# Fourier filter and SoLU network: filter products on VectorE in the first steps, weights prepared later, first sums ahead of loads

## The chip, the cores and the metric

The kernel runs on one core of a Trainium2 chip. The metric is the time of one execution on the device, in microseconds; the time of a kernel is the median over several runs. Besides, one execution of each kernel was taken by the hardware profiler, and all durations of single instructions come from such an execution.

## The reference

All data are 32-bit floats outside; x has 8 sequences of 3136 positions with 256 channels.

```
X = rfft(x, axis=1);  Y = X * (filt_r + 1j * filt_i)
y = irfft(Y, n=3136, axis=1)            # (8, 3136, 256) -> 25088 tokens of 256
h = y @ w_in                            # 256 -> 1024
sm = exp(h - max(h)) / (sum(exp(h - max(h))) + 1e-9)
solu = h * sm
ln = (solu - mean) / sqrt(var + 1e-6) * g_ln
out = ln @ w_out                        # 1024 -> 256
```

## The kernel before

**Transforms.** A sequence of 3136 = 49 x 64 positions is transformed in two stages with a pass through memory between them. For sequence 1 the first stage (L221) is done in 8 pieces of x; its results go to the memory tensor d (GpSimd issues the stores, L227). The second stage goes by units i = 0 to 6: a fetch of t from d (SP's queue, L286), the forward matmuls (L296, into two PSUM tiles pb), the product with the filter f (loaded by GpSimd's queue, L636), the inverse matmuls (L296 again, into pc, read from pr and pi), ScalarE's copy to g, and a store. From sequence 2 on the first stage works on a sum and a difference of two halves of x: diff on VectorE (L249), the sum on GpSimd (L255), matmuls at L264. Tables de come by ScalarE's queue (L677). At the end, matmuls (L367, L390) bring the data back into y, which stays in SBUF for two sequences.

**The filter product.** `multiply(i, part, add)` computes one part of the complex product: two multiplications on VectorE, each with one input in PSUM (L317, L318), then an add or subtract of two SBUF tensors (L319) on the engine that `add` names. Part 0 gives pr, part 1 gives pi; both use the same tile pt for the second term. Odd units of sequence 1 use spare room in y for t, f, pr, pi, pt, de and g, so their rows are named y.

**The network.** Tokens are taken in blocks of 128, two blocks (a pair) at a time. Both matrix products use seven block products instead of eight (Strassen's scheme in Winograd's form), so they need sums of inputs: `pair_sums` makes four sums of y on GpSimd (s, L696), `project_sums` those of solu (u, L696). `product(j, m)` is product m of pair j (L717); its PSUM banks are read by ScalarE (`keep`, L727) and by VectorE (`finish`, L741 and L738, which also track the row minimum nmax). Product 4 accumulates into the bank that `finish` of the same step reads first, and product 7 needs the bank that `finish` in the even step frees, so both wait for L741. Then `exponential` (ScalarE, L749), `normalize` (VectorE, L760 to L765), `turn` (a transpose in blocks of 32 on VectorE, L781), `square` (ScalarE, L773), `regroup` (SP's queue moves the transposed data into solu_t, L793), `deviations` (GpSimd, L800, L802) and, from step 9 on, `project` (L838).

**Order.** The order on every engine is written out by hand. `step(k)` emits one step; an even step k = 2j does products 1, 2, 6, 7 of pair j, an odd one products 5, 3, 4. Lists of jobs by step (`early`, `middle`, `late`, `stores`, `loads`, `products`, `first_parts`, `second_parts`) hang the work of the transforms into it. For sequence 1 the units 0 to 6 stand at steps t = 4, 5, 6, 7, 8, 10, 12 (`PLAN`): forward at t, part 0 of the product at the end of t, part 1 in step t + 1 (ahead of `turn` or after `normalize`), inverse late in t + 1. Fetches of t, de and f stand two steps ahead, f of odd units one step. LAG is 9: for t + 1 < 9, that is units 0 to 3, the add of `multiply` is on GpSimd; later, and for all other sequences, on VectorE.

**Before the steps.** The network's weights are given as 64-bit floats and converted by integer operations on VectorE (`load_float64`, L418 to L440) with a last add on GpSimd (L442), eight pieces in all, number 7 the last. `prepare_w_out` then works on w_out in four parts at the ends of steps 0 to 3: (0) scale by g_ln on VectorE (L654), (1) a mean by matmuls with ones (L662) and a copy to w_bar, (2) subtract w_bar on VectorE (L667), (3) the sums for Strassen's scheme on VectorE (`weight_sums`, L145). The tiles ones and w_bar take the buffers of pr and pi. The first reader of the finished w_out is `project` in step 9.

Loads of x whose step would be below 0 are issued at once while the lists are built, so ahead of everything in the steps; these are the two pieces 6 and 7 of sequence 1, four DMA issues on GpSimd's queue (L210). The first `pair_sums(0)` follows them in that queue.

Of the kernel before, what the change touches and what calls it, by code (L numbers as in the profile page):

```python
# [12 lines left out]
ALU = mybir.AluOpType  # L13
# [20 lines left out]
LAG = 9  # L34
# [60 lines left out]
def kernel(  # L95
# [10 lines left out]
    nc = tc.nc  # L106
# [72 lines left out]
    class Spectrum:  # L179
# [125 lines left out]
                                 t2[block, u::2, :])  # L305
            self.spectra[i] = pss

        def multiply(self, i, part, add):

            residues, w = self.shape(i)  # L310
            rows = slice(0, NQ * residues)
            f = self.fs[i][rows, 0:w]

            out, term = (self.buffer(i, kind, [P, 2, C])[rows, 0:w, :]
                         for kind in (("pr", "pi")[part], "pt"))
            re, im = (ps[rows, 0:w, :] for ps in self.spectra[i])
            nc.vector.tensor_tensor(out=out, in0=re, in1=f[:, :, part, :], op=ALU.mult)  # L317
            nc.vector.tensor_tensor(out=term, in0=im, in1=f[:, :, 1 - part, :], op=ALU.mult)  # L318
            add(out=out, in0=out, in1=term, op=(ALU.subtract, ALU.add)[part])  # L319
            self.prods.setdefault(i, []).append(out)  # L320
            if part == 1:
                del self.fs[i], self.spectra[i]
# [74 lines left out]
    with ExitStack() as st:  # L397
# [10 lines left out]
                in_=src)  # L408
            return raw

        def load_float64(dst, raw, negate, share):


            lo, hi = raw[:, :, 0], raw[:, :, 1]
            power = wpool.tile([P, 512], I32, name="power", tag="power", bufs=2)
            frac = dst.bitcast(I32)
            ts, stt = nc.vector.tensor_scalar, nc.vector.scalar_tensor_tensor
            ts(out=lo, in0=lo, scalar1=8, scalar2=None, op0=ALU.logical_shift_right)  # L418
            rest = lo.bitcast(FP32)
            ts(out=power, in0=hi, scalar1=20, scalar2=0x7FF, op0=ALU.logical_shift_right,  # L420
               op1=ALU.bitwise_and)
            ts(out=power, in0=power, scalar1=896.0, scalar2=0.0, op0=ALU.subtract, op1=ALU.max)
            if negate:
                ts(out=power, in0=power, scalar1=255.0, scalar2=None, op0=ALU.min)
                ts(out=power, in0=power, scalar1=23, scalar2=-2 ** 31, op0=ALU.logical_shift_left,
                   op1=ALU.bitwise_or)
            else:
                ts(out=power, in0=power, scalar1=255.0, scalar2=2.0 ** 23, op0=ALU.min, op1=ALU.mult)
            stt(out=power, in0=hi, scalar=-2 ** 31, in1=power, op0=ALU.bitwise_and,
                op1=ALU.bitwise_xor)  # L430
            ts(out=frac, in0=hi, scalar1=0xFFFFF, scalar2=3, op0=ALU.bitwise_and,
               op1=ALU.logical_shift_left)
            nc.vector.tensor_tensor(out=frac, in0=frac, in1=power, op=ALU.bitwise_or)


            if share:
                nc.scalar.mul(rest, lo, 2.0 ** -44)
                nc.gpsimd.tensor_tensor(out=rest, in0=rest, in1=power.bitcast(FP32), op=ALU.mult)
            else:
                stt(out=rest, in0=lo, scalar=2.0 ** -44, in1=power.bitcast(FP32), op0=ALU.mult,  # L440
                    op1=ALU.mult)
            nc.gpsimd.tensor_tensor(out=dst, in0=dst, in1=rest, op=ALU.add)  # L442

        filters, tables = {}, {}

# [23 lines left out]
        weights = []  # L469
# [17 lines left out]
        sp = Spectrum(0, pools, resident(filters), resident(tables))  # L487
        raws = {}
# [47 lines left out]
        idle_row(8, "idle")  # L536

        def convert(j):
            load_float64(weights[j][0], raws.pop(j), negate=j < 4, share=j < 4)

        for j in range(2):
            convert(j)
# [9 lines left out]
        for n in range(16):  # L552
            (nc.sync, nc.scalar)[n % 2].dma_start(
                out=t2_0[NH * (n % 4):NH * (n % 4) + NH, n // 4, :], in_=rows_x[n:n + 1])
# [29 lines left out]
        for i0, n, rows in ((0, 4, P), (4, 4, P), (8, NP - 9, P), (NP - 1, 1, NQ)):  # L584
            f, at = filters[i0]
            nc.sync.dma_start(
                out=f_dram[i0:i0 + n].rearrange("i u q k c -> (u q) i (k c)")[0:rows],
# [104 lines left out]
    def tokens(k, c):  # L692
        return y[:, c, P * (k % NT):P * (k % NT) + P]
# [4 lines left out]
    def pair_sums(j):  # L698

        s14 = upool.tile([P, 2, P], FP32, name=f"s14_{j}", tag="s14")  # L700
        s23 = wk.tile([P, 2, P], FP32, name=f"s23_{j}", tag="s23")
        sums[j] = s1, s2, s3, s4 = s14[:, 0, :], s23[:, 0, :], s23[:, 1, :], s14[:, 1, :]
        a11, a12, a21, a22 = (tokens(2 * j + i, c) for i in range(2) for c in range(KD))
        sum_of(s1, a21, a22, ALU.add)
        sum_of(s2, s1, a11, ALU.subtract)
        sum_of(s3, a11, a21, ALU.subtract)
        sum_of(s4, a12, s2, ALU.subtract)
# [164 lines left out]
    def ahead(t, by):  # L872
        return loads[max(0, t - by)]

    row_loads = []

    for e in range(1, B):
        first_at, spectrum_at, back_at = PLAN[e]
        sp = Spectrum(e, pools, load_filter, load_de)
        if e == 1:  # L880
            sp = second
            sp.load, sp.load_de = load_filter, load_de
        for i, t in enumerate(first_at):
            dma = nc.gpsimd.dma_start
            if e == 1:
                if i not in sp.xs:
                    row_loads.append((t, t - 1, -1, lambda sp=sp, i=i, dma=dma: sp.fetch_x(i, [dma] * 2)))
                for u in range(2):
                    (early, late)[u][t].append(lambda sp=sp, i=i, u=u: sp.first(
                        i, (u,), psum(f"pa_{sp.e}_{i}_{u}").rearrange("p a c -> p (a c)").rearrange(  # L890
                            "p (o n) -> p o n", o=1), nc.scalar.copy, sp.xs[i][0:NK, 2 * u:2 * u + 2, :]))
                    (early, late)[u][t].append(lambda sp=sp, i=i, u=u: sp.store_first(
                        i, 2 * u, nc.gpsimd.dma_start))
            else:

                row_loads.append((t, t - 2, -1, lambda sp=sp, i=i: sp.fetch_quarters(i, nc.sync.dma_start)))
                stores[t].append(lambda sp=sp, i=i: sp.difference(i))
                products[t].append(lambda sp=sp, i=i: sp.sum(i))
                late[t].append(lambda sp=sp, i=i: sp.first_quarters(
                    i, [psum(f"pa_{sp.e}_{i}_{g}") for g in range(2)]))  # L900
                stores[t + 1].append(lambda sp=sp, i=i, dma=dma: sp.store_quarters(i, dma))
        for i, t in enumerate(spectrum_at):

            other = e == 1 and i % 2 == 1 and t + 1 < LAG
            add = nc.gpsimd.tensor_tensor if t + 1 < LAG else nc.vector.tensor_tensor


            dma = nc.sync.dma_start if e == 1 else nc.scalar.dma_start
            ahead(t, 2).append(lambda sp=sp, i=i, dma=dma: sp.fetch(i, dma))
            ahead(t, 1 if e == 1 and i % 2 == 1 else 2).append(lambda sp=sp, i=i: sp.fetch_filter(i))  # L910
            ahead(t, 2).append(lambda sp=sp, i=i: sp.fetch_de(i))
            early[t].append(lambda sp=sp, i=i, o=other: sp.forward(i, psum_pair(f"pb_{sp.e}_{i}", o)))
            first_parts[t].append(lambda sp=sp, i=i, add=add: sp.multiply(i, 0, add))
            second_parts[t + 1].append(lambda sp=sp, i=i, add=add: sp.multiply(i, 1, add))
            late[t + 1].append(lambda sp=sp, i=i, o=other: sp.inverse(i, psum_pair(f"pc_{sp.e}_{i}", o)))
            stores[t + 2].append(lambda sp=sp, i=i: sp.store(i, nc.gpsimd.dma_start))


        assert S * (e - 1) <= P * (back_at[0] // 2 * 2) and P * (back_at[-1] + 2) <= S * e // P // 2 * 2 * P
        for ch, t in enumerate(back_at):  # L920
            row_loads.append((
                t, t - 1, spectrum_at[-1] + 2, lambda e=e, ch=ch: fetch_back(e, ch)))
            second_one = ch and t == back_at[ch - 1]
            (late if second_one else early)[t].append(lambda e=e, ch=ch: back_halves(
                e, ch, [psum(f"py_{e}_{ch}_{g}") for g in range(2)]))
            (late if second_one else middle)[t].append(lambda e=e, ch=ch: join_halves(e, ch))
    row_loads.sort(key=lambda load: load[0])
    for n, (t, latest, earliest, load) in enumerate(row_loads):


        at = max(t - 3, earliest, min(row_loads[n - 4][0] + 1, latest) if n >= 4 else -1)
        assert at < t
        if at < 0:
            load()
        else:
            loads[at].append(load)

# [2 lines left out]
    def step(k):  # L940
        j, odd = divmod(k, 2)
# [90 lines left out]
                job()  # L1032
        for job in late[k] + loads[k]:
            job()
        if k < 4:
            prepare_w_out(k)

    with tc.manual_schedule():
        pair_sums(0)
        for k in range(blocks + LAG):  # L1040
            step(k)

# [29 lines left out]
```

## Time and profile before

| | us |
|---|---|
| median of 6 runs (1636.37 to 1645.49) | 1640.63 |
| the profiled execution | 1628.72 |
| its span, first to last instruction | 1626.9 |
| TensorE busy | 1551.3 |
| VectorE busy | 1294.6 |
| GpSimd busy | 1130.8 |
| ScalarE busy | 901.7 |
| first product of step 0 starts (L717) | 105.34 |
| step 4 starts | 147.84 |
| step 9 starts | 200.37 |

In the profile's rows a line such as L296 is the line of the kernel that issued the instruction; the tiles written and read stand as out<-in; xN counts instructions that were merged. In a timeline the first two numbers are the start and the time that the row covers, and a bracket at the end gives the idle time of the engine before it and what ended it. In a row of a group, the numbers between bars are the sum of the durations in us and the mean in ns, and then the idle time before them. SPq and the like are queues from which an engine issues DMAs.

### The profile page before, as it was taken

What the parts mean: (1) busy time and instruction counts of PE and PEld (TensorE: products, weight loads), DVE (VectorE), ACT (ScalarE), POOL (GpSimd) and SP (SyncE); (2) the same over time, 40 slices, a digit from 0 to 9 for tenths busy, and PEclk for the clock granted to TensorE, in tenths of its full rate; (3) what the DMA queues carried; (4) which work ended last, traced back from release to release, by engine and by line L of the source; (5) the groups of instructions that cost most, each with busy time, mean ns of one, the idle gap of its engine ahead of it and who ended that gap; (6) DMA issues with size and microseconds to landing.
All of it is one profiled execution on the core that took longest, in us unless ns stands there. A gap on an engine that the chain in (4) does not pass through costs nothing. (4 is left out here: it accounts for less than half of the span.)

```text
span 1626.9 us, 36975 instructions
## 1 busy us (share of the span) xinstructions
PE 1551.3 (95%) x12710; PEld 1048.9 (64%) x12710; DVE 1294.6 (80%) x2633; ACT 901.7 (55%) x1772; POOL 1130.8 (70%) x1325
## 2 busy tenths in 40 slices
PE   5888799999999999999999999999999999999997
PEld 1353366666766676666766676666776777777776
DVE  1676598898899889887989789877888777777772
ACT  2134465566565665566656655566656555666562
POOL 4444687678777877697588867778576766676764
PEclk8999899999999999999999999999999999999999
DMA  9888768877888779866787678866785455444443
GB/s 271 252 258 246 214 205 223 235 222 193 207 241 241 196 182 248 229 190 174 203 248 208 178 190 232 229 178 170 204 230 160 122 132 127 102 111 111 105 111 98
DMA packets 377805, 312.13 MB, mean 192 GB/s; under 512 B 63322, under 2 KB 343395, under 8 KB 377619
## 3 DMA queue, kind: packets, MB, share of 16 engines
q1 hardware_dynamic: 306260, 169.81, 40.7%
q0 software_dynamic: 34464, 101.68, 20.6%
q10 hardware_dynamic: 36896, 38.28, 7.9%
q8 instruction: 103, 1.69, 0.5%
q14 instruction: 82, 0.67, 0.1%
HBM read 124.86 MB, written 81.50 MB: 127 GB/s over the span
## 5 line engine op out<-in xcount | busy, mean ns | idle before, releaser
L838 PEld LDWEIGHTS o<-w_out_sb,solu_t 128*128 128x128 f32 x3136 | 382.0, 193 | 48.2 <-issue 43.0
L838 PE MATMUL o<-w_out_sb,solu_t 128*128 128x128 f32 x3136 | 400.6, 276 | 3.1 <-DVE ot L854 2.7
L838 PEld LDWEIGHTS o<-w_out_sb,u 128*128 128x128 f32 x2352 | 308.1, 192 | 145.0 <-issue 104.8
L717 PE MATMUL m<-w_in_sb,s 128*128 128x512 f32 x784 | 395.9, 607 | 5.1 <-POOL s L696 1.6
L838 PE MATMUL o<-w_out_sb,u 128*128 128x128 f32 x2352 | 312.1, 276 | 8.5 <-ACT ot L850 5.9
L717 PE MATMUL m<-w_in_sb,y 128*128 128x512 f32 x588 | 309.5, 610 | 6.4 <-DVE nmax L741 4.4
L696 POOL TENSOR_TENSOR u<-solu_t 128x512 f32<-128x512 f32 x98 | 133.5, 1363 | 248.2 <-DMA solu_t<-turn 166.2
L727 ACT COPY h<-m 128x512 f32<-128x512 f32 x294 | 173.0, 589 | 238.2 <-PE m L717 214.8
L765 DVE SCALAR_TENSOR_TENSOR h<-e,rsum,h 128x1024 f32<-128x1024 f32 x196 | 287.3, 1466 | 6.9
L850 ACT ACTIVATE ot<-o,rs_t 128x128 f32<-128x128 f32 x392 | 143.8, 367 | 257.3 <-PE o L838 245.5
L741 DVE CUSTOM_DVE_ANT_0 h<-m,h 128x512 f32<-128x512 f32 x196 | 134.3, 685 | 162.6 <-ACT h L727 106.2
L773 ACT ACTIVATE h<-h,nmu 128x1024 f32<-128x1024 f32 x196 | 225.0, 1148 | 46.9 <-DVE turn L781 45.8
L781 DVE STREAM_TRANSPOSE turn<-h 128x1024 f32<-128x1024 f32 x196 | 243.1, 1240 | 3.2
L749 ACT ACTIVATE e<-h,nmax 128x1024 f32<-128x1024 f32 x196 | 225.3, 1150 | 5.0 <-DVE h L765 4.9
L717 PEld LDWEIGHTS m<-w_in_sb,s 128*128 128x128 f32 x784 | 128.7, 191 | 92.4 <-issue 81.6
L696 POOL TENSOR_TENSOR u<-solu_t,u 128x512 f32<-128x512 f32 x98 | 142.0, 1449 | 42.9 <-PE o L838 36.7
L717 PEld LDWEIGHTS m<-w_in_sb,y 128*128 128x128 f32 x588 | 96.5, 192 | 106.1 <-issue 54.5
L854 DVE SCALAR_TENSOR_TENSOR ot<-o,rs_t,ot 128x128 f32<-128x128 f32 x294 | 102.1, 347 | 78.7 <-ACT ot L850 57.0
L696 POOL TENSOR_TENSOR solu_t<-solu_t,solu_t 128x512 f32<-128x512 f32 x98 | 152.4, 1555 | 7.7
L696 POOL TENSOR_TENSOR u<-u,solu_t 128x512 f32<-128x512 f32 x98 | 133.4, 1361 | 0.6
L696 POOL TENSOR_TENSOR s<-y 128x128 f32<-128x128 f32 x196 | 100.8, 514 | 0.5
L367 PEld LDWEIGHTS py<-wb_t,t 50*64 50x64 f32 x3584 | 57.7, 135 | 43.3 <-issue 19.4
(113 smaller groups left out, 1971.4 us busy)
## 6 DMA issues: line engine op xcount, KB each, us to landing
solu_t<-turn SPq DMA_DIRECT2D x784, 128.0 KB
out_dram<-ot SPq DMA_DIRECT2D x196, 128.0 KB
t<-d POOLq DMA_DIRECT2D x112, 200.0 KB, 4.4
d<-x POOLq DMA_DIRECT2D x100, 200.0 KB, 5.2
f<-f_dram POOLq DMA_DIRECT2D x39, 512.0 KB, 7.7
d<-g POOLq DMA_DIRECT2D x39, 512.0 KB, 5.4
t<-d ACTq DMA_DIRECT2D x36, 512.0 KB
x<-in_x_dram SPq DMA_DIRECT2D x112, 98.0 KB
```

The lines of the kernel that those rows point to most:

```text
L367: nc.tensor.matmul(out=views[g][64 * h:64 * h + 64, cb, i, :], lhsT=t4[rows, i, c0:c0 + 64], rhs=wb_t[rows, 0:N1], start=True, stop=True)
L696: nc.gpsimd.tensor_tensor(out=out, in0=in0, in1=in1, op=op)
L717: nc.tensor.matmul(out=ms[j, bank], lhsT=lhsT, rhs=w_in_sb[:, w, :], start=m in (1, 2, 7), stop=True, skip_group_check=True)
L727: nc.scalar.copy(out=h_half(k, i), in_=ms[j, 0])
L741: nc.vector.tensor_tensor_reduce(out=h_half(k, i), in0=ms[j, bank], in1=h_half(*kept), scale=1.0, scalar=sofar, op0=ALU.add, op1=ALU.min, ...
L749: nc.scalar.activation(out=e, in_=hs[k], func=AFT.Exp, bias=nmaxs.pop(k)[:, 1:2], scale=-1.0, accum_out=esum)
L765: nc.vector.scalar_tensor_tensor(out=solu, in0=e, scalar=rsum, in1=solu, op0=ALU.mult, op1=ALU.mult, accum_out=nmu)
L773: nc.scalar.activation(out=solu, in_=solu, func=AFT.Square, bias=nmu, scale=-float(DFF), accum_out=variances[g][:, i:i + 1])
L781: nc.vector.transpose(out=turns[g][:, :, i, :], in_=solus[k].rearrange("p (f j) -> p f j", j=32))
L838: nc.tensor.matmul(out=pos[p, bank], lhsT=lhs[:, f, :], rhs=w[:, f, :], start=f == 0 and m in (1, 2, 7), stop=True, skip_group_check=True)
L850: nc.scalar.activation(out=out_half(p, *to)[0], in_=pos[p, 0], func=AFT.Copy, scale=rs)
L854: nc.vector.scalar_tensor_tensor(out=ot, in0=pos[p, bank], scalar=rs, in1=out_half(p, *kept)[0], op0=ALU.mult, op1=ALU.add)
```

## The change

Three things are changed, all of them in steps 0 to 9 or just ahead of them.

1. For units 0 to 3 of sequence 1, part 1 of the filter product is emitted directly after part 0, at the end of step t, and both adds are on VectorE. Units from 4 on, and the other sequences, stay as they were.
2. The parts of `prepare_w_out` stand at the ends of steps 0, 1, 3 and 5 instead of 0, 1, 2 and 3.
3. `pair_sums(0)` is emitted ahead of the two early loads of x, and the last add of weight piece 7 is on VectorE.

The instructions of TensorE, ScalarE and SP keep their order; GpSimd loses nine adds, and VectorE gains nine.

```diff
-        def multiply(self, i, part, add):
+        def multiply(self, i, part, add=nc.vector.tensor_tensor):
...
-        def load_float64(dst, raw, negate, share):
+        def load_float64(dst, raw, negate, share, add=nc.gpsimd.tensor_tensor):
...
-            nc.gpsimd.tensor_tensor(out=dst, in0=dst, in1=rest, op=ALU.add)
+            add(out=dst, in0=dst, in1=rest, op=ALU.add)
...
-            load_float64(weights[j][0], raws.pop(j), negate=j < 4, share=j < 4)
+            load_float64(weights[j][0], raws.pop(j), negate=j < 4, share=j < 4,
+                         add=(nc.vector if j == 7 else nc.gpsimd).tensor_tensor)
...
-    row_loads = []
+    row_loads, first_loads = [], []
...
-            add = nc.gpsimd.tensor_tensor if t + 1 < LAG else nc.vector.tensor_tensor
...
-            first_parts[t].append(lambda sp=sp, i=i, add=add: sp.multiply(i, 0, add))
-            second_parts[t + 1].append(lambda sp=sp, i=i, add=add: sp.multiply(i, 1, add))
+            first_parts[t].append(lambda sp=sp, i=i: sp.multiply(i, 0))
+            (first_parts[t] if t + 1 < LAG else second_parts[t + 1]).append(
+                lambda sp=sp, i=i: sp.multiply(i, 1))
...
-            load()
+            first_loads.append(load)
...
-        if k < 4:
-            prepare_w_out(k)
+        if k in (0, 1, 3, 5):
+            prepare_w_out((k + 1) // 2)
...
         pair_sums(0)
+        for load in first_loads:
+            load()
         for k in range(blocks + LAG):
```

## The prediction

> **What bounds it now.** I read the whole page first, then a table of stretches, then TensorE's timeline where the table shows a hole, then VectorE's and GpSimd's over the same time. (In the page's rows PE is TensorE, DVE VectorE, ACT ScalarE, POOL GpSimd.)
>
> ```profile
> PE 1551.3 (95%) x12710; PEld 1048.9 (64%) x12710; DVE 1294.6 (80%) x2633; ACT 901.7 (55%) x1772; POOL 1130.8 (70%) x1325
> PE   5888799999999999999999999999999999999997
> PEclk8999899999999999999999999999999999999999
> ```
>
> TensorE bounds the kernel: 95% busy, and from the sixth slice on (203 us) nothing is left to win. The change acts in steps 0 to 9, which lie between 105 and 203 us. There the table of stretches shows the holes (busy us of PE, PEld, DVE, ACT, POOL, then granted clock, DMA share, GB/s):
>
> ```profile
> 100.00:120.00 20.00, 16.29 (x68) 9.07 (x67) 13.75 (x34) 6.91 (x13) 10.04 (x15) 0.83 0.77 271
> 140.00:160.00 20.00, 15.87 (x68) 5.01 (x67) 19.46 (x40) 9.89 (x17) 8.21 (x11) 0.91 0.83 227
> 160.00:180.00 20.00, 15.02 (x78) 6.29 (x78) 12.12 (x25) 9.01 (x17) 15.05 (x18) 0.91 0.66 200
> 180.00:200.00 20.00, 12.83 (x63) 5.33 (x64) 13.21 (x24) 6.83 (x12) 13.43 (x15) 0.83 0.83 264
> 147.84:200.37 52.53, 38.49 (x200) 15.50 (x197) 37.75 (x71) 22.76 (x40) 33.73 (x37) 0.90 0.75 229
> 200.37:252.90 52.53, 51.95 (x334) 33.52 (x333) 44.91 (x89) 33.23 (x66) 43.40 (x52) 1.00 0.69 201
> ```
>
> In 147.84 to 200.37 us (start of step 4 to start of step 9) TensorE idles 14 us; right after, 0.6 us. No engine is full there, so these are waits in a chain. TensorE's timeline names them (in brackets the idle time and its releaser):
>
> ```profile
> 114.84 3.78 PE L717 MATMUL m<-w_in_sb,s 128*128 128x512 f32 x4 [1.63 <-POOL s L696]
> 144.20 2.07 PE L717 MATMUL m<-w_in_sb,y 128*128 128x512 f32 x2 [1.48 <-DVE nmax L741]
> 153.09 2.34 PE L717 MATMUL m<-w_in_sb,s 128*128 128x512 f32 x4 [1.17 <-DVE rsum L760]
> 164.25 0.44 PE L296 MATMUL pc<-pi,de 64*64 64x256 f32 x2 [4.85 <-POOL pi L319]
> 186.74 0.70 PE L296 MATMUL pc<-pi,de 64*64 64x256 f32 x2 [5.44 <-POOL pi L319]
> 197.43 1.58 PE L296 MATMUL pc<-y 64*64 64x256 f32 x8 [1.40 <-DVE y L317]
> ```
>
> So: the first sum of y comes late; step 3 waits for VectorE; twice the inverse transform waits for the last add of the filter product, which stands on GpSimd behind two loads of f, one sum of x and four sums of y. The stalls cost a second time through the clock: the granted clock is 0.50 in 113.4 to 120.2, 144.1 to 147.5, 164.6 to 168.0 and 185.0 to 191.9 us. TensorE at half speed for the parts of these in which it works loses about 2.7, 1.6, 1.7 and 2.6 us.
>
> VectorE meanwhile has holes of its own, because TensorE is late:
>
> ```profile
> 169.91 0.69 DVE L741 CUSTOM_DVE_ANT_0 h<-m,h 128x512 f32<-128x512 f32 x1 [5.30 <-PE m L717]
> 177.82 0.69 DVE L741 CUSTOM_DVE_ANT_0 h<-m,h 128x512 f32<-128x512 f32 x1 [2.30 <-ACT h L727]
> 193.22 0.69 DVE L741 CUSTOM_DVE_ANT_0 h<-m,h 128x512 f32<-128x512 f32 x1 [6.48 <-PE m L717]
> 202.15 0.69 DVE L741 CUSTOM_DVE_ANT_0 h<-m,h 128x512 f32<-128x512 f32 x1 [1.70 <-ACT h L727]
> ```
>
> **The first sums.** Now GpSimd does its last weight add (109.47 to 110.75), issues four loads of x (to 113.71), then the sums; TensorE gets the first at 114.84. After: that add is VectorE's (0.69 us by its two-SBUF-input rows L429 and L433 just before), GpSimd is free at 105.8, y is complete at 106.0, four sums of 0.46 end near 108. Product 6 then follows the transform of the last early x unit, which ends at 113.2: 1.63 us saved. The loads of x either start at 108 or, if what released them at 111.05 holds them, as now. They took 5.8 to 7.4 us to land, so by 120.3; their reader, now at 125.38, comes near 123. Cost nothing, cover 2.7 us. The extra 0.69 us on VectorE lies before a hole of 9.6 us (until 124.5): nothing.
>
> [...]
>
> **Step 3.** The subtraction of w_bar (4 x 0.684 = 2.5 us at 140.44) leaves VectorE's queue ahead of diff and of L741. L741 then waits for ScalarE's copy of h (140.89 + 0.58) instead: the 1.48 us go, and with them the fall at 144.1 (1.6 us, of which I count 0.9, for what remains of step 3 is short). Step 3 ends on VectorE (148.58 now) about 2.4 + 1.5 + 0.9 = 4.8 us sooner. The 1.17 us of step 4 stay: w_bar's 2.5 us stand exactly where the weight sums (4 x 0.687) stood.
>
> **Steps 4 to 9.** Gone from TensorE: 4.85, 5.44, 1.40 and three waits of 0.3 to 0.5 us, 12.8 in all, and the clock losses of 1.7 and 2.6. But they cannot all be won, since VectorE becomes the chain. Its stretch from 148.58 to 202.15 is 53.6 us, with holes of 5.30 + 2.30 + 6.48 + 1.70 + 0.3 = 16.1, so 37.5 of work. Added: eight adds (units 0 to 3, two each) and the four weight sums, now behind unit 1's products in step 5 (w_bar takes their old place): 8a + 2.7. Per step with an even unit the second products move ahead of diff and L741, where product 4 of the next step waits: TensorE's new stalls, about 2.5 us in steps 5 and 7, and in step 6, where products, weight sums and turn queue ahead of L741, 3 to 5 us before product 7.
>
> What is a? On GpSimd the add is 1.26 (1.68 when VectorE works beside it). On VectorE it is seen from step 8 on:
>
> ```profile
> L319 DVE TENSOR_TENSOR pr<-pr,pt 128x512 f32<-128x512 f32 x7 | 7.3, 1044 | 0.2
> L319 DVE TENSOR_TENSOR pi<-pi,pt 128x512 f32<-128x512 f32 x7 | 6.1, 872 | 0.2
> L319 DVE TENSOR_TENSOR y<-y 128x512 f32<-128x512 f32 x2 | 2.7, 1347 | 0.1
> ```
>
> 16 adds, 16.1 us: a = 1.0 (these rows reach to 420 us). [...] By the bare 0.69 the sum below would be 2.5 us better, by 2.5 (the longest add seen) it would be lost. I take 1.0, since GpSimd is no busier here (0.64 of the time) than later (0.83).
>
> Work is then 37.5 + 8.0 + 2.7 = 48.2, and if VectorE never waits, step 9's L741 comes 53.6 - 48.2 = 5.4 us sooner, plus 4.8 brought along: 10.2. Does anything make it wait? By walking the steps, TensorE stays ahead of VectorE at each L741 (its own gain at step 9 is 11 to 13). GpSimd loses about 12 us of adds and gets its loads of f out earlier: f of unit 1 no longer waits behind an add. After step 9 nothing is changed, and TensorE's 52 of 52.5 us busy carry the lead to the end.
>
> Unseen: how loads behave when 52.5 us of traffic at 0.75 share go into some 43. Bounds: nothing lost (20 us at 342 GB/s stand in this trace against 229 here), or 5 us (below). I take 0.2. Dropping w_out's preparation to steps 3 and 5 costs nothing more: its first reader is at 201.33. Nor does holding w_bar's buffer: unit 0's product writes it in step 4, after the subtraction on the same engine.
>
> **Sum.** 10 us. The profiled execution: 1628.7 (span 1626.9) to 1618.7. The median of the runs, 1640.63, lies 12 us above that execution; the holes are the kernel's own, so I subtract the same 10: **1630.6**.
>
> **Rivals.**
> *Loads set the pace* (0.22). turn of block 3 gates the rearranging of solu_t on SP, the deviations on GpSimd, and behind both t of unit 4 (issued 10.7 us after turn ended) and f of unit 3 (7.7 us to land). After the change turn(3) ends no sooner than now (164.6; the walk gives 166 to 168), while TensorE wants t of unit 4 near 180 instead of 193. 167 + 10.7 + 7 = 185: 5 us late. For it: the DMA share. Against: 4.6 us of the 10.7 were a wait for a load of de that will be earlier. Gain 5: 1635.6.
> *The holes only move* (0.12): the new stalls of steps 5 to 8 each drop the clock again, 4 x 1.7, and TensorE rather than VectorE ends late: gain 10 - 7 = 3 or less, 1638.
> *The shared port* (0.10), the slower side. The adds stand where GpSimd sums x, y and u. At a add of 2.0, and the six L765 each 0.6 longer (seen: 1.84 and 2.22 against 1.28), work grows by 16 + 2.7 + 3.6 = 22.3 against 16.1 of holes: 6.2 slower, 1646.8, if the lead of 4.8 is lost as well. With the lead, slower begins at a = 2.3. Only single adds reached that.
> The forecast has the remaining 0.56.
>
> **Range and chances.** The forecast alone, with a from 0.69 to 1.3 and the clock counted or not, spans gains of 7 to 15; should VectorE's time matter less than I think, all holes and clock losses are worth 24. Both sides with the loads' case: 1622 to 1638. About 0.3% (4.9 us) is what a measurement of this kernel can tell from no change. Faster than that: the forecast 0.56 and 0.14 of the loads' case, 0.70; within: 0.20; slower: 0.10.
>
> **What would show it.** TensorE's waits for POOL pi L319 and for POOL s at 114.84 are gone; steps 4 to 9 take some 47 us, not 52.5; VectorE is over 90% busy in them; new TensorE waits are for DVE L741. Adds on VectorE average 1.0 there. Wrong if waits for DMA (t, f, x) stand before L296 or L249, if adds average 2 us, or if the lead at step 9 is gone again by 300 us.

## The result and the profile after

| | before | after |
|---|---|---|
| median of the runs, us | 1639.13 (64 runs, 1628.3 to 1652.8) | 1633.16 (29 runs, 1623.6 to 1640.2) |
| the profiled execution, us | 1628.72 | 1629.19 |
| its span, us | 1626.9 | 1627.4 |
| steps 4 to 9, us | 52.53 | 46.71 |

The ratio is 0.9957 with a 95% interval of 0.9942 to 0.9972: 7.0 us less (4.6 to 9.5). The two medians of the table by themselves differ by 6.0. Ten us were forecast. The two profiled executions have the same length, which says nothing: single executions of one kernel scatter over some 20 us, three times the change.

The profile's page of after, busy times and then two rows of the 40 slices (40.7 us each):

```profile
PE 1546.6 (95%) x12710; PEld 1049.3 (64%) x12710; DVE 1297.0 (80%) x2642; ACT 903.0 (55%) x1772; POOL 1128.5 (69%) x1316
PE   5898789999999999999999999999999999999997
PEclk8999999999999999999999999999999999999999
```

The same matmuls keep TensorE busy 4.7 us less, which goes with the granted clock of the fifth slice (163 to 203 us): it went from 8 to 9. In the row of PE the third slice rose from 8 to 9, and the sixth (203 to 244 us), where before had no hole, fell from 9 to 8. A gain and a loss can be seen in these two rows. The table of stretches of after (busy us of PE, PEld, DVE, ACT, POOL, then granted clock, DMA share, GB/s); the first is step 4 to step 9, the second as much time behind it:

```profile
142.59:189.30 46.71, 32.83 (x200) 12.92 (x197) 45.95 (x87) 22.66 (x42) 22.34 (x29) 0.93 0.81 239
189.30:241.83 52.53, 47.39 (x292) 29.85 (x288) 38.96 (x76) 29.20 (x59) 37.29 (x45) 0.94 0.72 208
```

VectorE is busy 45.95 of 46.71 us in steps 4 to 9: 98%. It is the chain there, as the prediction had it. After step 9 TensorE is busy 47.4 of 52.5 us, where before had 52.0. TensorE's timeline of after names both:

```profile
121.77 2.67 PE L221 MATMUL pa<-x,wf_t 98*100 98x512 f32 x4 [1.56 <-DMA x<-in_x_dram]
148.66 2.33 PE L718 MATMUL m<-w_in_sb,s 128*128 128x512 f32 x4 [1.42 <-DVE rsum L761]
155.22 1.13 PE L718 MATMUL m<-w_in_sb,y 128*128 128x512 f32 x2 [2.13 <-DVE nmax L742]
167.51 2.05 PE L718 MATMUL m<-w_in_sb,s 128*128 128x512 f32 x2 [5.24 <-DVE rsum L761]
183.64 1.48 PE L296 MATMUL pb<-t,de 64*64 64x256 f32 x16 [4.48 <-issue]
210.40 1.16 PE L839 MATMUL o<-w_out_sb,solu_t 128*128 128x128 f32 x8 [1.69 <-DVE ot L855]
222.81 1.12 PE L296 MATMUL pb<-t,de 64*64 64x256 f32 x4 [3.03 <-DMA t<-d]
```

The waits for pi of 4.85 and 5.44 us and that for s are gone. In their place stand waits for VectorE (2.13 us in step 5, 5.24 us ahead of product 7 in step 6), then one for t of unit 4: the profile names no releaser for it, but unit 4 reads t and de alone, and its t was issued at 172.97, 1.65 us after its de. Behind step 9 come waits for t of unit 6 and for ot. The last is a load too, one engine on: in the chain of VectorE the row ahead of it waits for f.

```profile
207.30 0.69 DVE L317 TENSOR_TENSOR y<-pb,y 128x512 f32<-128x512 f32 x1 [2.87 <-DMA y<-f_dram]
```

**The lead, step by step.** Since spans scatter, I compare profiles from a common start: the first product of step 0, to the start of the transpose `turn` (L781) of blocks 6, 10 and 14, in steps 9, 13 and 17. Times in us; the lead is the row of before less that of the kernel.

| profile | to step 9 | to step 13 | to step 17 | rest of the span | lead at 9, 13, 17 |
|---|---|---|---|---|---|
| before | 100.43 | 133.33 | 166.98 | 1354.6 | |
| before, second profile | 100.40 | 134.07 | 169.60 | 1348.5 | 0.0, -0.7, -2.6 |
| after | 89.01 | 129.64 | 163.29 | 1358.4 | 11.4, 3.7, 3.7 |
| after, second profile | 91.93 | 129.02 | 165.23 | 1361.5 | 8.5, 4.3, 1.8 |

At step 9 the lead is 11.4 and 8.5 us (10.2 forecast). By step 13 two thirds and half of it are gone, but not to the same load. In the first profile 5.8 us go between steps 12 and 13, where t of unit 6 is late. In the second that load is in time, and 3.1 us go between steps 10 and 11, where f of unit 5 is late (VectorE's timeline of the second profile):

```profile
213.34 0.69 DVE L317 TENSOR_TENSOR y<-pb,y 128x512 f32<-128x512 f32 x1 [5.59 <-DMA y<-f_dram]
```

Not every later loss belongs to the change. The second profile of after loses 4.4 us between steps 14 and 15, and the second profile of before loses 3.5 us there as well: in both, ScalarE stands still for 5 to 6 us around its loads of t and de for sequence 2.

### The profile page after: what moved, and what is told of

Read it like the earlier page. It is cut to its first block, busy times and chain, and to the rows that moved or that the text cites. A ratio compares the mean times of both kernels' runs of the same rounds, so it can differ in the third digit from the quotient of the medians.

```text
span 1627.4 us, 36973 instructions
## 1 busy us (share of the span) xinstructions
PE 1546.6 (95%) x12710; PEld 1049.3 (64%) x12710; DVE 1297.0 (80%) x2642; ACT 903.0 (55%) x1772; POOL 1128.5 (69%) x1316
## 5 line engine op out<-in xcount | busy, mean ns | idle before, releaser
L718 PE MATMUL m<-w_in_sb,s 128*128 128x512 f32 x784 | 398.3, 609 | 9.7 <-DVE rsum L761 6.7
L718 PE MATMUL m<-w_in_sb,y 128*128 128x512 f32 x588 | 307.0, 605 | 4.0 <-DVE nmax L742 2.1
L742 DVE CUSTOM_DVE_ANT_0 h<-m,h 128x512 f32<-128x512 f32 x196 | 134.2, 685 | 152.8 <-ACT h L728 101.1
L718 PEld LDWEIGHTS m<-w_in_sb,s 128*128 128x128 f32 x784 | 129.2, 192 | 98.7 <-issue 89.1
L697 POOL TENSOR_TENSOR u<-solu_t,u 128x512 f32<-128x512 f32 x98 | 138.6, 1414 | 42.5 <-PE o L839 36.2
L718 PEld LDWEIGHTS m<-w_in_sb,y 128*128 128x128 f32 x588 | 96.4, 191 | 99.6 <-issue 55.2
L697 POOL TENSOR_TENSOR u<-u,solu_t 128x512 f32<-128x512 f32 x98 | 137.1, 1399 | 0.6
```

The lines of the kernel that those rows point to most:

```text
L697: nc.gpsimd.tensor_tensor(out=out, in0=in0, in1=in1, op=op)
L718: nc.tensor.matmul(out=ms[j, bank], lhsT=lhsT, rhs=w_in_sb[:, w, :], start=m in (1, 2, 7), stop=True, skip_group_check=True)
L742: nc.vector.tensor_tensor_reduce(out=h_half(k, i), in0=ms[j, bank], in1=h_half(*kept), scale=1.0, scalar=sofar, op0=ALU.add, op1=ALU.min, ...
```

## Experiments

Ratios are to runs of the kernel before on the same chip, with a 95% interval. In every kernel that keeps line numbers of before, L741 and L760 are what after has as L742 and L761.

**Each part alone.** The kernel before with only the first, only the second or only the third change. First part:

```diff
-            add = nc.gpsimd.tensor_tensor if t + 1 < LAG else nc.vector.tensor_tensor
...
-            first_parts[t].append(lambda sp=sp, i=i, add=add: sp.multiply(i, 0, add))
-            second_parts[t + 1].append(lambda sp=sp, i=i, add=add: sp.multiply(i, 1, add))
+            first_parts[t].append(lambda sp=sp, i=i: sp.multiply(i, 0))
+            (first_parts[t] if t + 1 < LAG else second_parts[t + 1]).append(
+                lambda sp=sp, i=i: sp.multiply(i, 1))
```

> Part 1 alone: both parts of the filter product of units 0 to 3 at the end of step t, adds on VectorE; w_out's preparation and the first sums as before. Theory A (the products carry the change): the two waits of some 5 us for GpSimd's add go, VectorE is without a hole from step 4 to 9, the lead over the kernel before at step 9 is 8 to 11 us, and the time is 0.2 to 0.5% shorter, about as with the whole change. Theory B (the clock and the start carry it): a lead of 3 us or less at step 9, no measurable change of the time.

Measured: 1633.66 us, ratio 0.9954 (0.9931 to 0.9976), lead 9.3, 6.2 and 2.7 us at steps 9, 13 and 17. The signs of theory A are there: both waits for pi are gone, and VectorE's longest hole in steps 4 to 8 is under 0.2 us. Within the intervals the products alone give what the whole change gives. Second part:

```diff
-        if k < 4:
-            prepare_w_out(k)
+        if k in (0, 1, 3, 5):
+            prepare_w_out((k + 1) // 2)
```

> Part 2 alone: w_out's preparation at the ends of steps 0, 1, 3 and 5. Theory A: the wait of 1.48 us in step 3 and the clock's fall after it go, 2 to 3 us of lead at step 4; the waits for GpSimd's add in steps 5 and 7 are still there, but the weight sums in step 5 fall into VectorE's hole, so a lead of 2 to 3 us at step 9 and 0 to 0.2% in time, within what can be told. Theory B: 5 us or more at step 9.

Measured: 1635.77 us, ratio 0.9976 (0.9958 to 0.9994), lead 2.6 at all three steps. The wait of 1.48 us in step 3 is gone. The two waits for the add on GpSimd stay, as theory A said, one of them shorter by 1.3 us (TensorE's timeline of this kernel):

```profile
161.90 0.70 PE L296 MATMUL pc<-pi,de 64*64 64x256 f32 x2 [3.58 <-POOL pi L319]
184.19 0.70 PE L296 MATMUL pc<-pi,de 64*64 64x256 f32 x2 [5.44 <-POOL pi L319]
```

Third part:

```diff
+            load_float64(weights[j][0], raws.pop(j), negate=j < 4, share=j < 4,
+                         add=(nc.vector if j == 7 else nc.gpsimd).tensor_tensor)
...
-            load()
+            first_loads.append(load)
...
         pair_sums(0)
+        for load in first_loads:
+            load()
```

> Part 3 alone: first sums of y ahead of the loads of x, last weight add on VectorE. Theory A: TensorE has no wait for the sum at 113 us, but the loads of x, landing no sooner, are waited for by the transform in step 1; lead of 1.5 to 2.5 us from step 2 on that stays to step 9; 0 to 0.15% in time. Theory B: 4 us or more at step 9 through the clock.

Measured: 1633.73 us, ratio 0.9966 (0.9940 to 0.9992). The wait for s is gone; the early loads of x now cost 0.25 and 0.37 us. The lead is 1.6 to 3.0 us up to step 8, near the 1.5 to 2.5 expected, but it does not last: 0.4 at step 9 and -0.9 at steps 13 and 17. In this profile TensorE was slow around a longer wait in step 3 (below): two matmuls of L718 took 2.07 us at 140.30 us and 2.08 at 144.21, against 1.02 at 121.82. The median came out better than expected, 0.34% (0.08 to 0.60) instead of 0 to 0.15%. The traced steps do not explain it.

```profile
140.30 2.07 PE L718 MATMUL m<-w_in_sb,y 128*128 128x512 f32 x2 [2.54 <-DVE nmax L742]
```

The ratios of the three add up to 17 us (0.46, 0.24 and 0.34%), the whole gives 7: the parts do not add. That they compete for the same slack behind step 9 is a likely reason, not a shown one.

**Another queue for t.** If it is the place of t in SP's queue that costs the lead (behind the rearranging of solu_t, the stores of out and loads of x), t by ScalarE's queue from unit 4 on should keep it.

```diff
-            dma = nc.sync.dma_start if e == 1 else nc.scalar.dma_start
+            dma = nc.sync.dma_start if e == 1 and i < 4 else nc.scalar.dma_start
```

> The whole change, and the loads of t of units 4, 5 and 6 issued by ScalarE's queue instead of SP's, where they stand behind the loads of solu_t, the store of rows and the stores of out. Theory A (the lead of 11 us at step 9 is lost at steps 8 to 12 to these loads' place in SP's queue): the waits of 4.5 us ahead of the forward transform in step 8 and of 3.0 us in step 12 shrink to under 1 us, the lead at step 13 rises from 3.3 to 9 us or more, and the time is 0.2 to 0.5% below the whole change's, so 0.6 to 0.9% below the kernel before. Theory C (the memory traffic as such is the limit): the waits stay, only with another load named, the lead at step 13 stays under 5 us, the time is as with the whole change.

Measured: 1634.21 us, ratio 0.9964 (0.9944 to 0.9983), lead 8.2, 2.6 and -0.1. Nothing won, and theory A, that the place in SP's queue alone costs the lead, is refuted. TensorE's timeline of this kernel:

```profile
155.12 2.01 PE L296 MATMUL pb<-y 64*64 64x256 f32 x16 [3.89 <-DMA y<-d]
186.12 1.12 PE L296 MATMUL pb<-t,de 64*64 64x256 f32 x16 [2.01 <-DMA de<-de_tbl]
```

The wait at unit 4 is shorter and now for the table de, which follows t in that queue. Ahead of it is one that after's first profile did not have: t of unit 1 (a tile in y) comes 3.9 us late in step 5. Behind step 9 VectorE waits 6.48 us for f of unit 5, and the lead falls from 8.1 us at step 10 to 2.2 at step 11. In a further kernel t goes by GpSimd's queue from unit 4 on, and f of odd units is fetched two steps ahead:

```diff
+            dma = (nc.sync if i < 4 else nc.gpsimd).dma_start if e == 1 else nc.scalar.dma_start
...
-            ahead(t, 1 if e == 1 and i % 2 == 1 else 2).append(lambda sp=sp, i=i: sp.fetch_filter(i))
+            ahead(t, 2).append(lambda sp=sp, i=i: sp.fetch_filter(i))
```

> [...] Theory A: the waits ahead of the forward transform in steps 8 and 12 under 1 us, no wait for f in step 10, lead at step 13 of 8 us or more, time 0.6 to 0.9% below the kernel before. Theory C: other loads are waited for, lead at step 13 under 5 us, time as with the whole change.

Measured: 1631.22 us, ratio 0.9957 (0.9936 to 0.9978), lead 7.3, 2.4 and 2.4. The waits for t of units 4 and 6 and for f are all gone, and the lead is lost none the less, as theory C said: 5.80 us to t of unit 1, and behind step 9 to a sum of x on GpSimd. That engine had stood still 6.24 us before, released by a DMA, ahead of the sums u of solu_t, which precede the sum of x in its queue (TensorE's timeline of this kernel, then GpSimd's).

```profile
156.38 2.01 PE L296 MATMUL pb<-y 64*64 64x256 f32 x16 [5.80 <-DMA y<-d]
213.05 0.71 PE L264 MATMUL pa<-x,wq_t 49*64 49x512 f32 x2 [3.54 <-POOL x L255]
```

```profile
206.30 2.29 POOL L697 TENSOR_TENSOR u<-solu_t 128x512 f32<-128x512 f32 x1 [6.24 <-DMA x<-in_x_dram]
```

**Less traffic.** If instead the DMA engines are short of time, taking bytes away should help after and not before. So both kernels ran with lighter loads of x:

```diff
+            again = self.e == 2 and i >= 4
+            out = held_x[i - 4] if again else self.pools["r"].tile(
+                [P, NCH, C], FP32, name=f"x_{self.e}_{i}", tag="r")
...
+            w = C // 4 if again else C
...
-                        dma(out=out[p:p + n, 2 * h:2 * h + 2, :],
+                        dma(out=out[p:p + n, 2 * h:2 * h + 2, 0:w],
...
-                                        ap=[[N2 * C, n], [step, 2], [1, C]]))
+                                        ap=[[N2 * C, n], [step, 2], [1, w]]))
```

> The kernel before with less traffic in steps 7 to 13: the loads of x for pieces 4 to 7 of sequence 2 keep their place and number but move a quarter of the channels (the rest of the tile keeps older values, so these pieces of the result are not the reference's). A control for the next run. All theories: steps 4 to 9 within 1 us of the kernel before, since its waits there are for GpSimd; time within 0.2%.

> The whole change with the same lighter loads of x (the same part of the result is not the reference's). Theory C (the traffic takes back the lead after step 9): the wait for t of unit 6 in step 12 goes, the lead over the control at step 13 is 8 us or more against 3.3 with full traffic, the time 0.6% or more below the control. Theory A (the place of t's loads in SP's queue takes it): the queue is the same, so the waits in steps 8 and 12 stay at 3 us or more and the lead at step 13 under 5 us.

Measured: before with light loads 1639.61 us, ratio 0.9999 (0.9981 to 1.0017); after with light loads 1632.36 us, ratio 0.9956 (0.9936 to 0.9976), its lead over the light kernel before 7.4, 6.3 and 2.3. The first lighter load is issued at 189.4 us (SP's queue), so the waits for t of unit 1 in step 5 (4.83 us) and of unit 4 in step 8 end before the edit acts, and this run cannot test them (TensorE's timeline, then SP's queue; here L302 is L296 and L246 is L240 of after):

```profile
189.06 1.56 PE L302 MATMUL pb<-t,de 64*64 64x256 f32 x11 [4.06 <-issue]
```

```profile
189.40 2.53 SPq L246 DMA_DIRECT2D x<-in_x_dram  x4
```

Where the edit acts, the rate was hardly lower (240 GB/s in 182 to 202 us and 186 in 202 to 242, against 236 and 190 in the first profile of after), but the waits for f of unit 5 and for t of unit 6 are not in this profile. From step 9 to step 13 only 1.1 us of the lead go, where the two profiles of after lost 7.7 and 4.2. That speaks for theory C, the traffic, behind step 9. But it is one profile, the rate does not show it, the lead of 6.3 us is short of the 8 that the theory asked for, and the ratio is no better than after's, so it is a hint and no proof.

**The weight sums later.** The last part of `prepare_w_out` at the end of step 7 instead of 5, to shorten VectorE's chain in step 6, where product 7 waits 5.24 us.

```diff
-        if k in (0, 1, 3, 5):
-            prepare_w_out((k + 1) // 2)
+        if k in (0, 1, 3, 7):
+            prepare_w_out(3 if k == 7 else (k + 1) // 2)
```

> The whole change, with the weight sums at the end of step 7 instead of step 5. The forecast's sum (VectorE is the chain from step 4 to 9): the wait of 5.2 us ahead of product 7 in step 6 falls to about 2.7, turn of block 3, the loads of solu_t and of t of unit 4 come 2.6 us sooner, and the 2.6 us come back as a wait ahead of product 7 in step 8, unless the wait for t of unit 4 hid them: lead at step 9 of 10 to 14 us. Time within 0.2% of the whole change.

Measured: 1630.74 us, ratio 0.9956 (0.9931 to 0.9981), lead 11.4, 7.5 and 7.5. The wait ahead of product 7 falls to 2.21 us, that for t of unit 4 rises to 5.65: one took the other's place, as expected.

```profile
164.55 1.10 PE L718 MATMUL m<-w_in_sb,s 128*128 128x512 f32 x2 [2.21 <-DVE rsum L761]
```

**The order of t of unit 1.** Over the profiles of kernels with after's order on SP's queue, t of unit 1 came late by 0, 3.95, 3.89, 4.83, 5.80 and 1.56 us. It is issued behind four loads of x; here one step sooner, ahead of them.

```diff
-            ahead(t, 2).append(lambda sp=sp, i=i, dma=dma: sp.fetch(i, dma))
+            ahead(t, 3 if e == 1 and i == 1 else 2).append(lambda sp=sp, i=i, dma=dma: sp.fetch(i, dma))
```

> The whole change, with the load of t of unit 1 directly behind that of unit 0 in SP's queue, ahead of the four loads of x for step 5, which stand between them now. Theory D, with the queue's order as the cause: the wait for t in step 5 is under 1 us, the lead at step 9 is 10 us or more, time 0.1 to 0.3% below the whole change. Theory D, with the traffic as the cause (loads move 390 GB/s at 148 to 152 us): the wait goes from t to x, that is to diff and the sum of x in step 5, the lead at step 9 is 4 to 9 us and the time as with the whole change.

Measured: 1635.30 us, ratio 0.9967 (0.9946 to 0.9989), lead 12.1, 9.5 and 6.4. SP's queue in the second profile of after, with the four loads of x ahead of t of unit 1 (a tile in y):

```profile
142.54 0.39 SPq L286 DMA_DIRECT2D t<-d  x1
142.98 2.05 SPq L240 DMA_DIRECT2D x<-in_x_dram  x4
145.14 0.39 SPq L286 DMA_DIRECT2D y<-d  x1
```

In this kernel the two loads of t follow each other directly, at 139.04 and 139.54 us. The wait is gone and the lead at step 9 is what theory D, with the order as the cause, asked for; the shorter time that it asked for does not show in the ratio. The wait is gone in the next kernel too, which has both edits of the last two experiments:

> The same with the weight sums at the end of step 7, the two edits that looked best. If the order in the queue is the cause: lead at step 9 of 12 us or more, at step 13 of 8 us or more, time 0.5 to 0.8% below the kernel before, the shortest of all. If the traffic is: as with the weight sums in step 7 alone, 0.44% below.

Measured: 1633.31 us, ratio 0.9957 (0.9932 to 0.9982), lead 3.9, 3.4 and 3.4, far from the 12 and 8 expected. This profile lost much of its lead in step 1, to an early load of x and a half clock behind it (granted clock 0.50 in 122 to 126 us; in the kernel of the experiment ahead of this one four such matmuls took 1.93 us at a granted clock of 1.00):

```profile
122.05 3.71 PE L221 MATMUL pa<-x,wf_t 98*100 98x512 f32 x4 [2.45 <-DMA x<-in_x_dram]
```

**The scatter.** After and before once more, unaltered.

> The whole change once more, unaltered, for a second profile of it and more runs. In four kernels that share its steps 0 to 5 to the letter, the forward transform of unit 1 in step 5 waited 1.6 to 5.8 us for its load of t, and in the first profile not at all. Theory D (this load lands on the edge, in some executions late): a wait between 0 and 6 us in step 5, a lead at step 9 of 11 us less about that wait. Theory E (the first profile shows the rule, the others were changed by their edits): no wait in step 5, lead 11 us again. Time 0.3 to 0.55% below the kernel before.

> The kernel before once more, unaltered: a second profile of it, and a comparison of a kernel with itself. From the start of step 0 the profiles of the whole change lead the first profile of before by 8 to 11 us at step 9 and by 2 to 4 us at step 17, while the medians differ by 6 to 7. If before's first profile was an ordinary one, its second has steps 0 to 17 within 1 us of it and the lead at step 17 is the true one; if it was a lucky one, the second takes 2 to 5 us more for these steps. Ratio of the medians 1.000, within 0.2%.

Measured: after 1634.92 us, ratio 0.9961 (0.9943 to 0.9979); before 1638.05 us, ratio 0.9988 (0.9969 to 1.0007). TensorE's timeline of the second profile of after, and then of before:

```profile
156.01 2.01 PE L296 MATMUL pb<-y 64*64 64x256 f32 x16 [3.95 <-DMA y<-d]
172.39 1.19 PE L718 MATMUL m<-w_in_sb,s 128*128 128x512 f32 x1 [4.63 <-DVE rsum L761]
188.27 1.12 PE L296 MATMUL pb<-t,de 64*64 64x256 f32 x16 [4.16 <-issue]
```

```profile
165.32 0.61 PE L296 MATMUL pc<-pi,de 64*64 64x256 f32 x2 [4.84 <-POOL pi L319]
187.81 0.70 PE L296 MATMUL pc<-pi,de 64*64 64x256 f32 x2 [5.43 <-POOL pi L319]
```

The two waits for GpSimd's add recur to 0.01 us in before (4.85 and 5.44 in its first profile). Those for loads change from one execution to the next: t of unit 1 was in time in the first profile of after. Before's first profile was a lucky one: the second takes 2.6 us more to step 17.

## Why the prediction was right and wrong

**Right: the mechanism up to step 9.** The waits for pi and for s went, and VectorE became the chain (98% busy, over 90% forecast). Steps 4 to 9 took 46.7 us (47 forecast), and the new waits stand behind L742, 2.13 us in step 5 (about 2.5) and 5.24 in step 6 (3 to 5). The lead brought along to step 4 was 5.6 us (4.8). The products alone reproduce the gain. The second profile is less close: 6.5 us of its lead stand at step 4, and steps 4 to 9 took 50.5 us, with VectorE busy 46.07 us of it (91%); there t of unit 1 was 3.95 us late. Over the eight profiles of kernels with all three changes these steps took 46.2 to 52.6 us, so the 46.7 is at the good end.

**The size of a.** I took 1.0 us for an add on VectorE, "since GpSimd is no busier here (0.64 of the time) than later (0.83)". The groups of VectorE between 150 and 182 us in after give 6.0 us for eight adds, 0.75 each (0.69 in the second profile):

```profile
L319 DVE TENSOR_TENSOR y<-y 128x512 f32<-128x512 f32 x4 | 3.2, 799 | 0.1
L319 DVE TENSOR_TENSOR pi<-pi,pt 128x512 f32<-128x512 f32 x2 | 1.4, 692 | 0.1
L319 DVE TENSOR_TENSOR pr<-pr,pt 128x512 f32<-128x512 f32 x2 | 1.4, 691 | 0.1
```

The busy share of GpSimd was the wrong measure. What counts is whether a GpSimd instruction is running when the add starts (VectorE's timeline of after, then GpSimd's):

```profile
187.31 1.77 DVE L319 TENSOR_TENSOR pr<-pr,pt 128x512 f32<-128x512 f32 x1
```

```profile
187.27 1.26 POOL L697 TENSOR_TENSOR u<-solu_t,u 128x512 f32<-128x512 f32 x1
```

GpSimd's sum ends at 188.53, and the add ends 0.55 us behind it, at 189.08. So it goes throughout: in the first profiles of before and after, between 140 and 360 us, VectorE has 40 such adds of 128x512. The 13 that began while GpSimd did no arithmetic took 0.69 us each. Of the others 25 ended 0.54 to 0.56 us after the GpSimd instruction that they had met, and two met one that was about to end and took 0.69. In those 25 the add thus lasted through the whole rest of GpSimd's instruction. Seven of the eight moved adds met none. Without its own adds GpSimd is busy 0.48 of steps 4 to 9 and stands waiting for long stretches (7.99 us for a load of x, 7.23 for ScalarE). The work was two us less than forecast, and the slower rival, "the shared port", is refuted for this kernel. No run shows a port, only the adds that lasted longer.

**Loads ahead of step 9.** "By walking the steps, TensorE stays ahead of VectorE at each L741" did not hold. In both profiles of after TensorE waited for t of unit 4 (4.48 and 4.16 us). In the first it was wanted at 183.64 - 4.48 = 179.2 us and there at 183.6; the rival of the loads said 180 and 185. In the seven profiles that have the products moved and this load in SP's queue, the wait is 3.6 to 5.7 us; in the three with before's order it is absent. In the second profile t of unit 1 was 3.95 us late as well, which no case named. These waits cost less than their length, since they lie in part beside VectorE's chain: at step 9 L742 of after waits 1.40 us. With the shorter adds the lead came out near 10 all the same, and that these two errors met is luck.

The early loads of x did not have the cover that was counted on. Their reader waited 1.56 us in after, and 0 to 2.45 us over the eight profiles. The prediction had them issued at 108 or 111 us. They were issued at 112.39, counted from the start of step 0 about 1 us later than before. GpSimd stood still for 2.63 us ahead of them, and the profile names as releaser the weight add (L442) that the change had moved to VectorE.

**The step that failed.** "After step 9 nothing is changed, and TensorE's 52 of 52.5 us busy carry the lead to the end." A stage without holes shows only that its loads were in time for the old pace; how much earlier they could have been wanted was not worked out. Eight to eleven us earlier, loads were late. The one that recurs is f of unit 5: VectorE waited for it 2.7 to 6.5 us in six of the eight profiles that have the products moved and fetch f of odd units one step ahead, and in none of the three with before's order. t of unit 6 was late by 3.03 us in the first profile of after, not at all in the second, and by 1.35 us in the second of before, so it is no sure mark of the change. After keeps 3.7 and 1.8 us at step 17.

What makes these loads late is not settled. With t on another queue the next load was late; with f fetched sooner as well, f was in time and a sum of x was 3.54 us late; with a lighter x behind step 9 most of the lead lasted to step 13, in one profile. f sooner by itself was not run. What the runs show is a row of loads with little slack each, of which the latest takes the lead.

**The clock.** Of the 4.8 us that the prediction brings along to step 4, the term of 2.4 is the wait of 1.63 us and 0.8 us for a half clock behind 113.4 us that ends sooner. No run shows that 0.8: in after the granted clock was 1.00 from 113.4 to 120.2 us, where before had 0.50. The falls at 164.6 and 185.0 became shorter in part: 0.50 stands in 167.2 to 170.6 and 184.3 to 187.7 us of after, 3.4 us each, against 3.4 and 6.9 before. The granted clock of steps 4 to 9 is 0.90 before and 0.93 in after, but 0.88, 0.87 and 0.91 in the three stretches of 20 us from 140 to 200 us of its second profile. New falls followed short waits, in after at 122.8 us (0.50 to 126.2 us) behind a gap of 1.56 us and at 221.8 us (0.50 to 228 us) within one of 3.03 us. In the kernel with t of unit 1 sooner a gap of 1.88 us at the same place left four such matmuls at 1.93 us and the granted clock at 1.00 (119 to 124 us). Nor did a fall follow after's gap of 2.13 us in step 5 (1.00 from 142.6 to 167.2 us).

The length of one gap therefore does not decide it; what does, these runs do not show.

**The rivals.** "The holes only move" (3 us or less) and "the shared port" (slower) lie outside the interval of 4.6 to 9.5. "Loads set the pace" (5 us) lies inside it and the forecast's 10 just outside: the true course is the forecast's to step 9 and the rival's from there, with f of unit 5 and others beside t of unit 4. In the sum for "the shared port", "slower begins at a = 2.3" leaves out the 3.6 us that the same rival counts for L765; with them it begins at 1.8.

**What stays open.** At step 17 the whole change leads by 1.8 to 6.3 us in the profiles (two of after, 163.3 and 165.2, against three with the kernel before's order, 167.0, 168.8 and 169.6), 4.2 in the mean; the ratio says 7.0 (4.6 to 9.5). The rest of the span ran from 1348.5 to 1372.8 us over all the profiles, whatever the edit, so where the other 3 us are, or whether they are, cannot be read from single profiles. Nor do the leads of the variants show in their ratios: 6.4 and 7.5 us at step 17 for two of them stand beside 0.9967 and 0.9956, and the third part alone has 0.9966 with a lead of -0.9. No variant is measurably better than the change.

## What to carry to other kernels

When a stall is removed ahead of loads whose places in the queues stay as they were, the gain is worth what the loads of the following steps have in slack (of after's lead of 11.4 us at step 9, 3.7 were left at step 13): for each one, take the time from its landing to its first reader before adding the gain through to the end. When work moves from one engine to another, judge contention by what the first engine will be running at the moments when the moved work starts, not by its busy share (an add took 0.69 us where it met no arithmetic of GpSimd, and 1.77 in step 8 of after, where it met a sum). For changes under 1%, compare the way from a common start, step by step and over several profiles; the span of one says nothing.

## What the runs showed of the hardware

- An add of two SBUF tensors (128x512, f32) on VectorE took 0.69 us when it began while GpSimd did no arithmetic (13 cases between 140 and 360 us of before and after). When it met a running GpSimd sum it finished 0.54 to 0.56 us behind that one's end (25 of 27 cases; 1.77 us in step 8 of after). The same add on GpSimd took 1.26 to 1.71 us in steps 4 to 8 of before.
- A load of the same size, issued at the same place in a queue, met its reader 0 to 5.8 us late over six profiles with one order, while the two waits for GpSimd's add recurred to 0.01 us in before.
- A gap of 1.56 us in TensorE's work was followed by half clock (granted clock 0.50 in 124 to 126 us of after); one of 1.88 us in the kernel with t of unit 1 sooner was not (1.00 in 119 to 124 us).
